# A decode kernel whose MLP and attention results are summed in one PSUM: biases by small matmuls, gates folded into the operands, last V load in two halves, one output transfer

## The chip, the cores and the metric

The kernel runs on 1 core of one Trainium2 chip. The metric is device time in microseconds (us). All runs here are of state "fast", so they can be compared with each other.

## The reference

A gated mix of one decode step of attention and an MLP, for 8 sequences of one token each:

```python
# B=8, Sq=1, D=576, H=32, Sk=4096, Dh=128, F=4608, all inputs bf16
g = sigmoid((x * gate_w).sum(-1, keepdims=True))
q = (x @ wq) per head;  p = softmax(q . k_cache * Dh**-0.5);  a = (p . v_cache) @ wo
h = gelu(layernorm(x) @ w1 + b1);                             b = h @ w2 + b2
out = g * a + (1 - g) * b
```

The K and V caches are 268 MB each. Everything else is small: 4.7 MB each for wq and wo, 5.3 MB each for w1 and w2.

## The kernel before

SBUF has three large slots of 64 KB per partition. wq, w1 and w2 are loaded into them first. Then come K and V of 32 groups (8 heads of one sequence each) in rotation, and at the end wo. All large loads are issued on one queue, and each load waits until its slot is free:

```python
land[kind, g] = op("sync", lambda e: e.dma_start(slot[s][:, :, :], src), free[n - 3], dma=dma)
# free after: up-projection (slot 1), down-projection (slot 2), scores of a group (K), eviction of O (V)
```

The MLP runs once, ahead of the first group. Its biases are broadcast to 8 partitions in four column quarters by eight small transfers, and VectorE adds them:

```python
ld_b1 = [load("scalar", b1_4[32 * i:32 * i + B, :], bcast(B_b1, i * FC, FC), ...) for i in range(4)]
ld_b2 = [load("scalar", b2_4[32 * i:32 * i + B, :], bcast(B_b2, i * QN, QN), ...) for i in range(4)]
for k in range(3):
    for c in range(4):                      # column group c of TensorE: PSUM partitions 32c..32c+7
        for kt in range(NKT):               # 5 matmuls, 8 columns of weights, 384 of data
            matmul(up_ps[k][32 * c:32 * c + B, 0:FB], lhsT=yT_sb[:, yi, :], rhs=w1..., start=(kt == 0), stop=(kt == NKT - 1))
    hb = up_ps[k] + b1_4; ...               # GELU in three parts
...
bmg = (y_ps + b2_4) * (1 - g)               # MLP result, kept in SBUF
```

A group then goes through scores (VectorE multiplies, TensorE sums), softmax, exponentials, 64 PV matmuls, eviction, row sums and gather, normalisation, and a copy into OT. (PV is the product of the softmax weights P with V; eviction is the copy of its result O from PSUM to SBUF; OT holds O of all groups, transposed for the product with wo.) The end of the kernel is:

```python
pv(last); evict(last); gather(last)         # gather begins with the row sums
norm(last)                                  # sum, reciprocal, On, OTs
place_o("vector", last - 1, last + 1)       # OT
for j in range(NJO):                        # 32 x 4 matmuls with wo, which arrives in pieces of 24, 6 and 2 j
    p_a = quarters(OT[:, j, :], wo_sb[:, j, :], j == 0, j == NJO - 1, [ld_wo[j], ...])
out_sb = y_ps * g4[:, 0:1] + bmg_sb         # one VectorE instruction on 104 partitions
ld_out = [load(("sync", "scalar")[i % 2], out_flat[:, i * QN:(i + 1) * QN], out_sb[32 * i:32 * i + B, :], ...) for i in range(4)]
```

## Time and profile before

| | before |
|---|---|
| time, median of the first three runs | 1296.77 us (1296.72 to 1297.39) |
| span of the profiled run | 1295.0 us |
| bytes moved, mean rate | 557.22 MB, 430 GB/s |
| busy share: TensorE, VectorE, ScalarE | 56%, 63%, 12% |

These are the lines of part 2 of the page. Each line has 40 slices of the span, and a digit is the busy share in tenths:

```profile
PE   2366466455556555556555556555556555556645
DVE  3387667655667665567665567765567765567762
DMA  9999999999999999999999999999999999999998
```

No compute engine is near full, and the DMA is at 9 tenths in all slices but the last. The loop is set by bytes: a change can gain only where the DMA stream is held up, and after it has ended.

The next lines are the end of the timeline. The columns are start in us, duration, engine, line, operation, tiles, count, and in brackets the idle time before it and what ended it:

```profile
1280.36 6.01 PE L617 MATMUL PS<-SL,P 128*32 128x512 bf16 x64 [2.67 <-DMA SL<-in_A_v_cache_dram]
1286.43 0.60 ACT L623 ACTIVATE O_sb<-PS 128x512 f32<-128x512 f32 x1 [10.82 <-PE PS L617]
...
1287.16 1.04 PE L632 MATMUL PS<-O_sb,selq 128*32 128x128 f32 x8
...
1289.72 2.17 PE L525 MATMUL PS<-SL,OT 128*8 128x144 bf16 x128 [1.51 <-DVE OT L656]
1291.94 0.37 DVE L727 SCALAR_TENSOR_TENSOR out_sb<-PS,g,bmg_sb 104x144 bf16<-104x144 f32 x1 [2.37 <-PE PS L525]
1292.34 0.72 SPq L320 DMA_DIRECT2D out_dram<-out_sb  x2
1292.34 0.65 ACTq L320 DMA_DIRECT2D out_dram<-out_sb  x2
```

This is a chain from the landing of the last V (1280.3) to the output. The 128 matmuls with wo were released by OT, which is compute. The chain does not show how close the wo load was behind. In the trace's landing records (when a transfer's semaphore tells that its data are there), the last of wo's three pieces landed at 1291.33, only 0.58 us before those matmuls were done.

In the prologue, the up-projection of the kernel before:

```profile
27.91 5.25 PE L496 MATMUL PS<-SL 128*8 128x384 bf16 x60 [7.79 <-DMA SL<-in_B_w_dram]
```

### The profile page before, as it was taken

To read this page: it belongs to the slowest core of one execution; us is meant where nothing else is said; L and a number is where in the kernel's file an instruction comes from. 1 tells how busy PE (TensorE), PEld (TensorE's weight loads), DVE (VectorE), ACT (ScalarE), POOL (GpSimd) and SP (SyncE) were. 2 spreads that over 40 slices of the span, in tenths; PEclk is the share of its full clock that TensorE was granted. 3 is DMA by queue.
4 is the path that set the end of the run, shared out by engine and by line. 5 is a ranking of instruction groups with operands and counts; after the bars stand their busy time and mean duration, and the time that the engine had idled before them with its cause. 6 is when DMAs were issued, how large, how long until landed. Compare 5 with 4: busy or idle time off the path is not lost.

```text
span 1295.0 us, 11764 instructions
## 1 busy us (share of the span) xinstructions
PE 720.0 (56%) x4902; PEld 333.8 (26%) x4902; DVE 821.5 (63%) x884; ACT 160.9 (12%) x587; POOL 41.0 (3%) x60
## 2 busy tenths in 40 slices
PE   2366466455556555556555556555556555556645
PEld 1222223122223122223222223222223222223223
DVE  3387667655667665567665567765567765567762
ACT  1011110111110111110011110011111011111011
POOL 1001000000000000000000000000000000000000
PEclk8698888877898787899788899878888877888888
DMA  9999999999999999999999999999999999999998
GB/s 395 437 428 440 430 436 430 433 435 433 433 431 435 437 429 433 433 435 437 425 437 435 433 431 431 437 435 431 435 429 437 435 427 435 435 435 431 429 439 343
DMA packets 10605, 557.22 MB, mean 430 GB/s; under 512 B 1328, under 2 KB 1344, under 8 KB 1888
## 3 DMA queue, kind: packets, MB, share of 16 engines
q1 hardware_dynamic: 10400, 556.93, 99.5%
q8 instruction: 9, 0.15, 0.0%
q10 hardware_dynamic: 192, 0.11, 0.0%
q14 instruction: 4, 0.03, 0.0%
HBM read 557.03 MB, written 0.01 MB: 430 GB/s over the span
## 4 chain that ended last, share of the span: by engine, by line
DMA 57%; DVE 23%; PE 13%; ACT 5%; issue 1%; ACTq 0%; SPq 0%
DMA SL<-in_A_k_cache_dram 53%; DVE SL L561 19%; PE PS L566 7%; PE PS L617 5%; ACT P L606 4%; DVE s_sb L572 4%; DMA SL<-in_A_v_cache_dram 3%; DMA SL<-in_A_wq_dram 1%; PE PS L632 1%; ACT O_sb L623 1%; PE PS L478 0%; PE PS L628 0%; PE PS L525 0%; SPq L320 0%; DVE OTs L646 0%
## 5 line engine op out<-in xcount | busy, mean ns | idle before, releaser
L566 PE MATMUL PS<-SL,ident 128*128 128x512 bf16 x2048 | 546.9, 419 | 530.3 <-DVE SL L561 530.3
L561 DVE TENSOR_TENSOR SL<-SL,q_bc 128x4096 bf16<-128x4096 bf16 x256 | 581.5, 2282 | 320.6 <-DMA SL<-in_A_k_cache_dram 320.6
L566 PEld LDWEIGHTS PS<-SL,ident 128*128 128x128 bf16 x2048 | 198.9, 106 | 865.3 <-DVE SL L561 627.4
L572 DVE TENSOR_REDUCE s_sb<-PS 128x32 f32<-128x512 f32 x256 | 175.1, 684 | 89.9 <-PE PS L566 89.7
L606 ACT ACTIVATE P<-s_sb,hb 128x256 bf16<-128x256 f32 x256 | 126.2, 494 | 663.2 <-PE PS L617 645.6
L617 PE MATMUL PS<-SL,P 128*32 128x512 bf16 x2048 | 127.9, 387 | 2.7 <-DMA SL<-in_A_v_cache_dram 2.7
L617 PEld LDWEIGHTS PS<-SL,P 128*32 128x32 bf16 x2048 | 95.8, 152 | 21.1 <-DMA SL<-in_A_v_cache_dram 3.1
L545 POOL TENSOR_SCALAR Qm<-Q,sel 128x256 bf16<-128x256 bf16 x33 | 34.2, 1036 | 908.1 <-ACT O_sb L623 845.4
L553 ACT ACTIVATE q_bc<-PS 128x128 bf16<-128x128 f32 x33 | 9.2, 278 | 418.2 <-PE PS L550 418.2
L606 ACT ACTIVATION_READ_ACCUMULATOR P<-s_sb,hb 128x1 f32 x256 | 47.8, 187 | 0.0
L632 PE MATMUL PS<-O_sb,selq 128*32 128x128 f32 x256 | 34.1, 278 | 0.0
L632 PEld LDWEIGHTS PS<-O_sb,selq 128*32 128x32 f32 x256 | 26.1, 113 | 0.2
L623 ACT ACTIVATE O_sb<-PS 128x512 f32<-128x512 f32 x32 | 18.4, 575 | 10.8 <-PE PS L617 10.8
L639 DVE TENSOR_REDUCE zs<-PS 32x1 f32<-32x8 f32 x32 | 4.7, 147 | 17.3 <-PE PS L632 17.3
L591 DVE TENSOR_REDUCE mA<-s_sb 128x1 f32<-128x256 f32 x32 | 13.4, 420 | 1.1
L656 POOL CAST OT<-OTs 32x96 bf16<-32x96 f32 (+2 forms) x12 | 3.8, 319 | 320.2 <-DVE OTs L646 320.1
L646 DVE TENSOR_REDUCE OTs<-On 32x32 f32<-32x128 f32 x32 | 11.9, 371 | 1.1
L642 DVE SCALAR_TENSOR_TENSOR On<-PS,rz,dqm 32x128 f32<-32x128 f32 x32 | 10.8, 339 | 1.2
L500 DVE TENSOR_TENSOR SL<-PS,SL 104x384 f32<-104x384 f32 x3 | 1.7, 552 | 15.3 <-PE PS L496 15.3
L628 PE MATMUL PS<-acc,hsel 128*32 128x8 f32 x64 | 7.4, 187 | 5.4 <-ACT O_sb L623 5.4
L496 PE MATMUL PS<-SL 128*8 128x384 bf16 x60 | 5.2, 492 | 7.8 <-DMA SL<-in_B_w_dram 7.8
L628 PEld LDWEIGHTS PS<-acc,hsel 128*32 128x32 f32 x64 | 4.4, 109 | 19.0 <-issue 12.7
(72 smaller groups left out, 107.9 us busy)
## 6 DMA issues: line engine op xcount, KB each, us to landing
SL<-in_B_w_dram SPq DMA_DIRECT2D x1, 5184.0 KB, 38.2
SL<-in_B_w_dram SPq DMA_DIRECT2D x1, 4608.0 KB, 24.6
SL<-in_A_wq_dram SPq DMA_DIRECT2D x1, 4096.0 KB, 13.0
SL<-in_A_wo_dram SPq DMA_DIRECT2D x1, 3456.0 KB, 21.9
SL<-in_A_wo_dram SPq DMA_DIRECT2D x1, 864.0 KB, 23.6
SL<-in_B_w_dram SPq DMA_DIRECT2D x1, 576.0 KB, 25.6
SL<-in_A_wq_dram SPq DMA_DIRECT2D x1, 512.0 KB, 14.2
SL<-in_A_k_cache_dram SPq DMA_DIRECT2D x32, 43.4
```

What stands on the lines that cost most here:

```text
L545: g_qm[g] = op("gpsimd", lambda e: e.tensor_scalar(out=Qm[:, :, :].rearrange("p k d -> p (k d)"), in0=Q4[:, 2 * hg * DH:(2 * hg + 2) * DH] ...
L561: v_mult[g, c] = op("vector", lambda e: e.tensor_tensor(out=part, in0=part, in1=qb, op=ALU.mult), [land["k", g], a_qb[g]], token="tensor" ...
L566: p_sum[g, c] = op("tensor", lambda e, r=r, n=n: e.matmul(tr_ps[par][:, :], lhsT=ident[:, :], rhs=r, start=(n == 0), stop=(n == NCH - 1)), ...
L572: v_red[g, c] = op("vector", lambda e: e.tensor_reduce(out=s_sb[:, c * CT:(c + 1) * CT], in_=tr_ps[par][:, :].rearrange("p (t c) -> p t c" ...
L591: t = op("vector", lambda e: e.tensor_reduce(out=mA[:, 0:1], in_=s_sb[:, :], axis=AX.X, op=ALU.max), [v_red[g, NCK - 1], c_mA], token=own)
L606: a_exp[g] = op("scalar", lambda e, h=h: e.activation(out=P[:, h, :], in_=s_sb[:, :], func=ACT.Exp, bias=hb8[:, h:h + 1], scale=1.0, accum ...
L617: p_pv[g] = op("tensor", lambda e, o=o, tq=tq: e.matmul(o, lhsT=P[:, :, :].rearrange("p h t -> p (h t)")[:, tq::NTQ], rhs=vb[:, tq::NTQ, : ...
L623: a_ev[g] = op("scalar", lambda e: e.activation(out=O_sb[:].rearrange("p t d -> p (t d)"), in_=o_ps[:, :], func=ACT.Copy), [p_pv[g], p_z.g ...
L628: p_z[g] = op("tensor", lambda e: e.matmul(oz_ps[0:32, DH:DH + HB], lhsT=hsel[:, :], rhs=acc[:, place(g), :], start=True, stop=True), [a_e ...
L632: p_oz[g] = op("tensor", lambda e, tt=tt: e.matmul(oz_ps[0:32, 0:DH], lhsT=selq[:, tt, :], rhs=O_sb[:, tt, :], start=(tt == 0), stop=(tt = ...
L642: t = op("vector", lambda e: e.scalar_tensor_tensor(out=On[:, :].rearrange("p (q j) -> p q j", q=NDQ), in0=oz_ps[0:32, 0:DH].rearrange("p ...
L646: v_norm[g] = op("vector", lambda e: e.tensor_reduce(out=OTs[:, :, place(g + 2)], in_=On[:, :].rearrange("p (q j) -> p j q", q=NDQ), axis= ...
```

## The change

Intent: take work off the end. The MLP stays in PSUM, and attention is added to it there. To allow that, (1-g) is folded into h, and g into O when OT is made. One evicted tile then goes out in one transfer. b1 enters as matmuls with a single row; b2, still broadcast to 8 partitions but in one transfer, enters as four fp32 matmuls that apply (1-g). So two small transfers take the place of the eight. The last V comes in two halves, so that its PV can begin early, and the row sums of the last group are made before its PV.

```diff
-    ld_b1 = [load("scalar", b1_4[32 * i:32 * i + B, :], bcast(B_b1, i * FC, FC), f"ld_b1{i}", [c_b1]) for i in range(4)]
-    ld_b2 = [load("scalar", b2_4[32 * i:32 * i + B, :], bcast(B_b2, i * QN, QN), f"ld_b2{i}", [c_b2]) for i in range(4)]
+    ld_b1 = load("scalar", b1_row, <one row of F>, "ld_b1")
+    ld_b2 = load("scalar", b2_8, bcast(B_b2, 0, D), "ld_b2")
...
+        if (kind, g) == ("v", NG - 1):
+            land[kind, g] = [<two loads, one per half>]
...
     for k in range(3):
         for c in range(4):
             for kt in range(NKT):
-                ... start=(kt == 0), stop=(kt == NKT - 1))
+                ... start=(kt == 0), stop=False)
-        <bias add and GELU of this third on VectorE>
+            p_up = op("tensor", lambda e, o=o, col=col: e.matmul(
+                o, lhsT=one1[:, :], rhs=b1_row[:, col:col + FB], start=False, stop=True), [ld_b1, c_one1])
+    <GELU of all 1152 columns at once, last factor times g4[0:QP, 1:2]>
...
+    for i in range(4):      # b2 times (1-g), fp32, into the same PSUM
+        p_b2 = matmul(y_ps[32 * i:32 * i + B, 0:QN], lhsT=diag2[:, 1, :], rhs=b2_f[:, i * QN:(i + 1) * QN], start=False, stop=False)
-    v_bx = ...; v_bmg = ...
...
+    row_sums(last); inverse(last)
     pv(last); evict(last); gather(last); norm(last); place_o("vector", last - 1, last + 1)    # place_o multiplies by g32
-        p_a = quarters(OT[:, j, :], wo_sb[:, j, :], j == 0, j == NJO - 1, ...)
+        p_a = quarters(OT[:, j, :], wo_sb[:, j, :], False, j == NJO - 1, ...)
+    parts = <four copies PSUM to out_sb [8, 576], two on VectorE, two on ScalarE>
+    ld_out = [load("sync", out_flat, out_sb[:, :], "ld_out", parts)]
```

(Cut. The exponentials also write P in two halves of the keys, so that the first 32 PV matmuls need only the first half of V.)

More of the change, by code (lines that the diff above doesn't have):

```diff
@@ L264, in bass_gated_mix__mha_block_cached__mixer_channel_mlp__decode_kernel @@
     late = Tail(2, NJ * D)
-    b1_4 = late.take([128, FC])
+    b1_row = late.take([1, F])
     hrow = late.take([128, FC])
     hT_sb = late.take([128, NJ, B])
-    hb = late.take32([128, FC])
+    b2_8 = late.take([B, D])
+    b2_f = late.take32([B, D])
     t2 = late.take32([128, FC])
-    b2_4 = sb("b2_4", [128, QN], BF16)
     Q4 = sb("Q4", [128, (H // 4) * DH], BF16)
@@ L284, in bass_gated_mix__mha_block_cached__mixer_channel_mlp__decode_kernel @@
     OT = sb("OT", [128, NJO, B], BF16)
-    bmg_sb = sb("bmg_sb", [128, QN], F32)
-    out_sb = sb("out_sb", [128, QN], BF16)
+    out_sb = sb("out_sb", [B, D], BF16)
+    spread8 = sb("spread8", [B, 128], F32)
+    ones8 = sb("ones8", [B, 32], F32)
+    one1 = sb("one1", [1, B], BF16)
+    diag2 = sb("diag2", [B, 2, B], F32)
     g4 = sb("g4", [128, 2], F32)
+    g32 = sb("g32", [32, 2, B], F32)
     ident = sb("ident", [128, 128], BF16)
@@ L298, in bass_gated_mix__mha_block_cached__mixer_channel_mlp__decode_kernel @@
     hb8 = sb("hb8", [128, HB], F32)
-    P = sb("P", [128, HB, NTT], BF16)
+    P = sb("P", [128, 2, HB, NTT // 2], BF16)
     O_sb = sb("O_sb", [128, TQ, DH], F32)
@@ L310, in bass_gated_mix__mha_block_cached__mixer_channel_mlp__decode_kernel @@
     y_ps = bank[7]
-    up_ps = [bank[4], bank[5], bank[6]]
+    up_ps = PS[:, 4 * 512:7 * 512].rearrange("p (k n) -> p k n", k=3)
+    g4_ps = bank[3][:, 0:2]
+    g32_ps = bank[3][0:32, 64:64 + 2 * B]
     ht_ps = PS[:, 0:NJ * 32].rearrange("p (j c b) -> p j c b", j=NJ, c=4)
@@ L339, in bass_gated_mix__mha_block_cached__mixer_channel_mlp__decode_kernel @@
     ld_w2 = load("sync", w2_sb, B_w2.rearrange("(p j) n -> p j n", j=NJ), "ld_w2")
-    c_b2 = op("gpsimd", lambda e: e.memset(b2_4[:], 0.0))
-    c_g4 = op("gpsimd", lambda e: e.memset(g4[:], 0.0))
-    c_b1 = op("gpsimd", lambda e: e.memset(b1_4, 0.0))
     ld_x = load("scalar", x_sb, x_flat, "ld_x")
     ld_gw = load("scalar", gw8, bcast(gate_w, 0, D), "ld_gw")
-    ld_b1 = [load("scalar", b1_4[32 * i:32 * i + B, :], bcast(B_b1, i * FC, FC), f"ld_b1{i}", [c_b1]) for i in range(4)]
-    ld_b2 = [load("scalar", b2_4[32 * i:32 * i + B, :], bcast(B_b2, i * QN, QN), f"ld_b2{i}", [c_b2]) for i in range(4)]
+    ld_b1 = load("scalar", b1_row, bass.AP(tensor=B_b1.tensor, offset=B_b1.offset, ap=[[F, 1], [1, F]]), "ld_b1")
+    ld_b2 = load("scalar", b2_8, bcast(B_b2, 0, D), "ld_b2")
     def kv_src(cache, g):
@@ L370, in load_kv @@
         used_in = g if kind == "k" else g + 1
+        if (kind, g) == ("v", NG - 1):
+            land[kind, g] = [load("sync", slot[s][:, i * NTT // 2:(i + 1) * NTT // 2, :],
+                                  src[:, i * NTT // 2:(i + 1) * NTT // 2, :], f"ld_v{g}_{i}", free[n - 3]) for i in range(2)]
+            return n
         if in_loop(used_in):
@@ L377, in load_kv @@
         land[kind, g] = op("sync", lambda e: e.dma_start(slot[s][:, :, :], src), free[n - 3], dma=dma)
+        if kind == "v":
+            land[kind, g] = [land[kind, g]] * 2
         return n
@@ L410, in bass_gated_mix__mha_block_cached__mixer_channel_mlp__decode_kernel @@
         in_=bass.AP(tensor=sel32, offset=0, ap=[[pstride(sel32), 128], [1, TQ], [TQ, HB], [0, NDQ]])), [c_sel32])
+    c_one8 = memset("gpsimd", ones8[:], 1.0)
+    c_one1 = memset("gpsimd", one1[:], 1.0)
+    c_b2 = op("gpsimd", lambda e: e.tensor_copy(out=b2_f, in_=b2_8), [ld_b2])
+    c_sp8 = op("vector", lambda e: e.tensor_copy(
+        out=spread8[:].rearrange("b (c r) -> b c r", c=4),
+        in_=bass.AP(tensor=ident, offset=0, ap=[[pstride(ident), B], [0, 4], [1, 32]])), [c_id])
     c_Rows = op("vector", lambda e: e.tensor_reduce(
@@ L461, in bass_gated_mix__mha_block_cached__mixer_channel_mlp__decode_kernel @@
                                                    scalar1=-1.0, scalar2=1.0, op0=ALU.mult, op1=ALU.add), [a_g])
-    for i in range(4):
-        v_g4 = op("vector", lambda e, i=i: e.tensor_copy(out=g4[32 * i:32 * i + B, :], in_=stat[:, G_COL:G_COL + 2]),
-                  [v_omg, c_g4])
+    v_dg = op("vector", lambda e: e.tensor_tensor(
+        out=diag2[:], in0=bass.AP(tensor=ident, offset=0, ap=[[pstride(ident), B], [0, 2], [1, B]]),
+        in1=bass.AP(tensor=stat, offset=G_COL, ap=[[pstride(stat), B], [1, 2], [0, B]]), op=ALU.mult), [v_omg, c_id])
     v_yz = spread(yz, y_sb, [v_y])
@@ L467, in bass_gated_mix__mha_block_cached__mixer_channel_mlp__decode_kernel @@
     v_yT = untransposed(yT_sb, YT_COL, [p_yT])
+    t = op("tensor", lambda e: e.matmul(g4_ps, lhsT=spread8[:, :], rhs=stat[:, G_COL:G_COL + 2], start=True, stop=True),
+           [v_dg, c_sp8])
+    t = op("tensor", lambda e: e.matmul(g32_ps, lhsT=ones8[:, :], rhs=diag2[:].rearrange("k s b -> k (s b)"),
+                                        start=True, stop=True), [c_one8])
+    v_g4 = op("vector", lambda e: e.tensor_copy(out=g4[:, :], in_=g4_ps), [t])
+    v_g32 = op("vector", lambda e: e.tensor_copy(out=g32[:].rearrange("p s b -> p (s b)"), in_=g32_ps), [t])
     a_Q = []
@@ L484, in bass_gated_mix__mha_block_cached__mixer_channel_mlp__decode_kernel @@
     load_kv("k", 0)
-    v_hb, v_hrow = [], []
     for k in range(3):
-        p_up = None
         for c in range(4):
+            col = c * FC + k * FB
+            o = up_ps[32 * c:32 * c + B, k, 0:FB]
             for kt in range(NKT):
-                o = up_ps[k][32 * c:32 * c + B, 0:FB]
-                col = c * FC + k * FB
                 r = w1_sb[:, kt, col:col + FB] if kt < NKF else w1_t[:, col - (c // 2) * (F // 2):][:, 0:FB]
@@ L496, in bass_gated_mix__mha_block_cached__mixer_channel_mlp__decode_kernel @@
                 p_up = op("tensor", lambda e, o=o, r=r, kt=kt, yi=yi: e.matmul(
-                    o, lhsT=yT_sb[:, yi, :], rhs=r, start=(kt == 0), stop=(kt == NKT - 1)),
+                    o, lhsT=yT_sb[:, yi, :], rhs=r, start=(kt == 0), stop=False),
                     [v_yT, *ld_w1, *c_ps] if c == kt == k == 0 else ())
-        cs = slice(k * FB, (k + 1) * FB)
-        v_hb.append(op("vector", lambda e, k=k, cs=cs: e.tensor_tensor(
-            out=hb[0:QP, cs], in0=up_ps[k][0:QP, 0:FB], in1=b1_4[0:QP, cs], op=ALU.add), [p_up, *ld_b1]))
@@ L502, in bass_gated_mix__mha_block_cached__mixer_channel_mlp__decode_kernel @@
-        t = op("vector", lambda e, cs=cs: e.tensor_tensor(out=t2[0:QP, cs], in0=hb[0:QP, cs], in1=hb[0:QP, cs],
-                                                          op=ALU.mult), [v_hb[k]])
-        t = op("vector", lambda e, cs=cs: e.tensor_scalar(out=t2[0:QP, cs], in0=t2[0:QP, cs], scalar1=0.044715,
-                                                          scalar2=1.0, op0=ALU.mult, op1=ALU.add), [t])
-        t = op("vector", lambda e, cs=cs: e.tensor_tensor(out=t2[0:QP, cs], in0=t2[0:QP, cs], in1=hb[0:QP, cs],
-                                                          op=ALU.mult), [t])
@@ L508, in bass_gated_mix__mha_block_cached__mixer_channel_mlp__decode_kernel @@
-        t = op("scalar", lambda e, cs=cs: e.activation(out=t2[0:QP, cs], in_=t2[0:QP, cs], func=ACT.Sigmoid,
-                                                       scale=gelu_c), [t])
-        v_hrow.append(op("vector", lambda e, cs=cs: e.tensor_tensor(
-            out=hrow[0:QP, cs], in0=hb[0:QP, cs], in1=t2[0:QP, cs], op=ALU.mult), [t]))
-    free[1] = [p_up]
+            p_up = op("tensor", lambda e, o=o, col=col: e.matmul(
+                o, lhsT=one1[:, :], rhs=b1_row[:, col:col + FB], start=False, stop=True), [ld_b1, c_one1])
@@ new lines, in bass_gated_mix__mha_block_cached__mixer_channel_mlp__decode_kernel @@
+    free[1] = [p_up]
+    h = up_ps[0:QP, :, 0:FB]
+    t3 = t2[0:QP, :].rearrange("p (k n) -> p k n", k=3)
+    t = op("vector", lambda e: e.tensor_copy(out=t3, in_=h), [p_up])
+    t = op("vector", lambda e: e.tensor_tensor(out=t3, in0=t3, in1=h, op=ALU.mult), [t])
+    t = op("vector", lambda e: e.tensor_scalar(out=t3, in0=t3, scalar1=0.044715, scalar2=1.0, op0=ALU.mult, op1=ALU.add), [t])
+    t = op("vector", lambda e: e.tensor_tensor(out=t3, in0=t3, in1=h, op=ALU.mult), [t])
+    t = op("scalar", lambda e: e.activation(out=t3, in_=t3, func=ACT.Sigmoid, scale=gelu_c), [t])
@@ L514, in bass_gated_mix__mha_block_cached__mixer_channel_mlp__decode_kernel @@
+    v_h = op("vector", lambda e: e.scalar_tensor_tensor(
+        out=hrow[0:QP, :].rearrange("p (k n) -> p k n", k=3), in0=h, scalar=g4[0:QP, 1:2], in1=t3,
+        op0=ALU.mult, op1=ALU.mult), [t, v_g4])
+    v_hb, v_hrow = [v_h], [v_h]
     per_quarter = bass.AP(tensor=ident, offset=0, ap=[[pstride(ident), QP], [32, 4], [1, B]])
@@ L530, in bass_gated_mix__mha_block_cached__mixer_channel_mlp__decode_kernel @@
     for jt in range(NJ):
-        p_down = quarters(hT_sb[:, jt, :], w2_sb[:, jt, :], jt == 0, jt == NJ - 1,
+        p_down = quarters(hT_sb[:, jt, :], w2_sb[:, jt, :], jt == 0, False,
                           [ld_w2, *v_hT, v_yT] if jt == 0 else ())
-    v_bx = op("vector", lambda e: e.tensor_tensor(
-        out=bmg_sb[0:QP, :], in0=y_ps[0:QP, 0:QN], in1=b2_4[0:QP, :], op=ALU.add), [p_down, *ld_b2])
-    v_bmg = op("vector", lambda e: e.tensor_scalar(
-        out=bmg_sb[0:QP, :], in0=bmg_sb[0:QP, :], scalar1=g4[0:QP, 1:2], scalar2=None, op0=ALU.mult), [v_bx, v_g4])
-    free[2] = [p_down]
-    a_qb, v_mult, v_red, p_sum, v_nm, a_exp, p_pv, a_ev, p_z, p_oz, v_norm, g_ot, g_qm, p_q = ({} for _ in range(14))
+    for i in range(4):
+        p_b2 = op("tensor", lambda e, i=i: e.matmul(
+            y_ps[32 * i:32 * i + B, 0:QN], lhsT=diag2[:, 1, :], rhs=b2_f[:, i * QN:(i + 1) * QN], start=False, stop=False),
+            [c_b2, v_dg])
+    free[2] = [p_b2]
+    a_qb, v_mult, v_red, p_sum, v_nm, a_exp, p_pv, a_ev, p_z, p_oz, v_norm, g_ot, g_qm, p_q, v_rz = ({} for _ in range(15))
     def q_of(g):
@@ L606, in exps @@
             a_exp[g] = op("scalar", lambda e, h=h: e.activation(
-                out=P[:, h, :], in_=s_sb[:, :], func=ACT.Exp, bias=hb8[:, h:h + 1], scale=1.0,
+                out=P[:, :, h, :], in_=s_sb[:, :].rearrange("p (s t) -> p s t", s=2), func=ACT.Exp, bias=hb8[:, h:h + 1], scale=1.0,
                 accum_out=acc[:, place(g), h:h + 1]),
@@ L613, in pv @@
         vb = slot[at_slot["v", g]]
+        flat = P[:, :, :, :].rearrange("p s h t -> p (s h t)")
         for tq in range(NTQ):
+            s, i = divmod(tq, NTQ // 2)
             o = o_ps[32 * (tq % 4):32 * (tq % 4) + TQ * HB, :]
-            w = [land["v", g], a_exp[g] if g < G0 - 1 else a_ev[g - 1], a_ev.get(g - 1), *v_hT] if tq == 0 else ()
-            p_pv[g] = op("tensor", lambda e, o=o, tq=tq: e.matmul(
-                o, lhsT=P[:, :, :].rearrange("p h t -> p (h t)")[:, tq::NTQ], rhs=vb[:, tq::NTQ, :],
-                start=(tq < 4), stop=(tq >= NTQ - 4)), w,
+            lhsT = flat[:, s * HB * NTT // 2 + i:(s + 1) * HB * NTT // 2:NTQ // 2]
+            rhs = vb[:, s * NTT // 2 + i:(s + 1) * NTT // 2:NTQ // 2, :]
+            w = [land["v", g][s], a_exp[g] if g < G0 - 1 else a_ev[g - 1], a_ev.get(g - 1), *v_hT] if i == 0 else ()
+            p_pv[g] = op("tensor", lambda e, o=o, lhsT=lhsT, rhs=rhs, tq=tq: e.matmul(
+                o, lhsT=lhsT, rhs=rhs, start=(tq < 4), stop=(tq >= NTQ - 4)), w,
                 token="scalar" if in_loop(g + 1) and tq == NTQ - 1 else None)
@@ L624, in evict, with row_sums @@
                                                       func=ACT.Copy), [p_pv[g], p_z.get(g - 1)])
+    def row_sums(g):
+        p_z[g] = op("tensor", lambda e: e.matmul(
+            oz_ps[0:32, DH:DH + HB], lhsT=hsel[:, :], rhs=acc[:, place(g), :], start=True, stop=True),
+            [a_ev[g] if g < NG - 1 else a_ev[g - 1], v_norm.get(g - 1), c_hsel, *v_hb])
     def gather(g):
         looped = in_loop(g + 2)
-        p_z[g] = op("tensor", lambda e: e.matmul(
-            oz_ps[0:32, DH:DH + HB], lhsT=hsel[:, :], rhs=acc[:, place(g), :], start=True, stop=True),
-            [a_ev[g], v_norm.get(g - 1), c_hsel, *v_hb])
         for tt in range(TQ):
@@ L633, in gather, with inverse @@
                 oz_ps[0:32, 0:DH], lhsT=selq[:, tt, :], rhs=O_sb[:, tt, :], start=(tt == 0),
-                stop=(tt == TQ - 1)), [c_selq] if tt == 0 else (),
+                stop=(tt == TQ - 1)), [a_ev[g], c_selq, v_rz.get(g)] if tt == 0 else (),
                 token="vector" if looped and tt == TQ - 1 else None)
+    def inverse(g):
+        own = "vector" if in_loop(g + 2) else None
+        t = op("vector", lambda e: e.tensor_reduce(out=zs[:, :], in_=oz_ps[0:32, DH:DH + HB], axis=AX.X, op=ALU.add),
+               [p_oz.get(g, p_z[g])], token=own)
+        v_rz[g] = op("vector", lambda e: e.reciprocal(out=rz[0:32, :], in_=zs[:, :]), [t], token=own)
     def norm(g):
         own = "vector" if in_loop(g + 2) else None
-        t = op("vector", lambda e: e.tensor_reduce(out=zs[:, :], in_=oz_ps[0:32, DH:DH + HB], axis=AX.X, op=ALU.add),
-               [p_oz[g]], token=own)
-        t = op("vector", lambda e: e.reciprocal(out=rz[0:32, :], in_=zs[:, :]), [t], token=own)
         t = op("vector", lambda e: e.scalar_tensor_tensor(
@@ L644, in norm @@
             scalar=rz[0:32, 0:1], in1=bass.AP(tensor=dqm, offset=0, ap=[[pstride(dqm), 32], [1, NDQ], [0, NJO]]),
-            op0=ALU.mult, op1=ALU.mult), [t, c_dqm], token=own)
+            op0=ALU.mult, op1=ALU.mult), [v_rz[g], p_oz[g], c_dqm], token=own)
         v_norm[g] = op("vector", lambda e: e.tensor_reduce(
@@ L655, in place_o @@
             n = min(g1 - g, B - b)
-            t = g_ot[g0] = op(engine, lambda e, hg=hg, b=b, n=n, at=g - g0: e.tensor_copy(
-                out=OT[32 * hg:32 * hg + 32, :, b:b + n], in_=OTs[:, :, at:at + n]), [v_norm[g1 - 1], t])
+            t = g_ot[g0] = op(engine, lambda e, hg=hg, b=b, n=n, at=g - g0: e.tensor_tensor(
+                out=OT[32 * hg:32 * hg + 32, :, b:b + n], in0=OTs[:, :, at:at + n],
+                in1=bass.AP(tensor=g32, offset=b, ap=[[pstride(g32), 32], [0, NJO], [1, n]]), op=ALU.mult),
+                [v_norm[g1 - 1], v_g32, t])
             g += n
@@ L696, in bass_gated_mix__mha_block_cached__mixer_channel_mlp__decode_kernel @@
         if in_loop(g):
+            row_sums(g - 2)
             gather(g - 2)
@@ L706, in bass_gated_mix__mha_block_cached__mixer_channel_mlp__decode_kernel @@
         if in_loop(g):
+            inverse(g - 2)
             norm(g - 2)
@@ L716, in bass_gated_mix__mha_block_cached__mixer_channel_mlp__decode_kernel @@
     last = NG - 1
+    row_sums(last - 1)
     gather(last - 1)
+    inverse(last - 1)
     norm(last - 1)
+    row_sums(last)
+    inverse(last)
     pv(last)
@@ L724, in bass_gated_mix__mha_block_cached__mixer_channel_mlp__decode_kernel @@
     for j in range(NJO):
-        p_a = quarters(OT[:, j, :], wo_sb[:, j, :], j == 0, j == NJO - 1,
-                       [ld_wo[j], v_bx, *g_ot.values()])
-    t = op("vector", lambda e: e.scalar_tensor_tensor(
-        out=out_sb[0:QP, :], in0=y_ps[0:QP, 0:QN], scalar=g4[0:QP, 0:1], in1=bmg_sb[0:QP, :],
-        op0=ALU.mult, op1=ALU.add), [p_a, v_bmg])
-    ld_out = [load(("sync", "scalar")[i % 2], out_flat[:, i * QN:(i + 1) * QN], out_sb[32 * i:32 * i + B, :],
-                   f"ld_out{i}", [t]) for i in range(4)]
+        p_a = quarters(OT[:, j, :], wo_sb[:, j, :], False, j == NJO - 1, [ld_wo[j], *g_ot.values()])
+    parts = [op("vector" if i < 2 else "scalar", lambda e, i=i: (e.tensor_copy if i < 2 else e.copy)(
+        out_sb[:, i * QN:(i + 1) * QN], y_ps[32 * i:32 * i + B, 0:QN]), [p_a]) for i in range(4)]
+    ld_out = [load("sync", out_flat, out_sb[:, :], "ld_out", parts)]
     op("sync", lambda e: None, ld_out)
```

## The prediction

> What bounds the kernel: the DMA. In the page's 40 slices its share is 9 tenths nearly throughout, 430 GB/s over a span of 1295.0 us; TensorE is 56% busy, VectorE 63%. The DMA queue's waits show the next K or V load always issued while an earlier one is still moving (last K: issued at 1198.4, landed at 1241.6). So the 32 loop passes are set by bytes, and the change leaves those bytes alone. Only the start and the end can move the time.
>
> Start. Up-projection, GELU and down-projection run from 27.9 to 49.2 us in the timeline, but the first K lands only at 60.45, so some 10 us are slack. The 12 bias matmuls, the joined 1152-column VectorE chain and 4 fp32 matmuls for b2 may add about 4 us: hidden. The V load that waits for the down-projection has 30 us of slack. The broadcast bias rows go from 64 packets to a few: at most 0.4 us of some engines' time (2304-byte packets took about 0.095 us each, 32 of them on a part of the engines), so 0 to 0.4 us of the stream's end.
>
> End, from the timeline and the chain of waits: last V landed 1280.32; 64 PV matmuls to 1286.4, mostly at half clock; eviction 0.61; row sums 0.23; gather 0.91; sum and reciprocal 0.37; On, OTs, OT 0.95; Wo matmuls 1289.72 to 1291.91; output 0.37; four output transfers; end 1295.0. The chain names these steps, so on paper V in halves and early row sums take off 1.5 to 3 us (the first half should land about 9.7 us earlier, so TensorE can start once the head before has been gathered and normalised, about 1279). But Wo's three pieces land at 1288.57, 1290.64 and 1291.33 (DMA landings in the trace), just behind the chain. They queue behind V and do not come earlier. So Wo's matmuls can't finish before about 1291.5, and the new chain turns into a wait for Wo: nearly all the gain of the halves is lost, 0.4 us at most remain.
>
> Worse, TensorE will now idle 1.5 to 3 us before Wo's first piece. The Trainium skill, TensorE: Matmul & The Clock Gate, Part 1, says the clock is judged over free-running windows of about 3.4 us and halves after an idle one; here the granted clock was 0.50 from 1274.9 to 1285.1 (three such windows) and 1.0 after. If it falls again, Wo's 128 matmuls cost 31 ns each (as the down-projection's 144 did, 4.49 us) instead of 17, and end near 1292.5: 0.6 us later than now.
>
> Output: two VectorE copies in parallel with two ScalarE copies of 8x144, estimated at 0.5 us against 0.37 now; one transfer saves the second issue on each queue, 0.35 to 0.4 us (first transfers landed 1293.55 and 1293.76, second ones 1293.96 and 1294.16). Net about -0.25 us.
>
> Sum: -0.25 (output), 0 to -0.4 (start), -0.4 to +0.6 (Wo at full or half clock): about -0.6 us of 1296.77. Predicted 1296.2 us, range 1295.2 to 1297.2; faster by over 2% 0.005, within 2% 0.99, slower 0.005.
>
> What would show it: DMA slices unchanged; the chain's end names the Wo load ahead of the last matmuls; PV ends 1 to 2.5 us earlier while Wo's matmuls start at the landing of Wo's first piece (about 1288.6); one output transfer. Wrong if Wo lands earlier or later with V in halves, if the second half of V waits for something new, if the strided P slows PV inside the loop (slack about 13 us per V load), or if the HBM rate differs between runs by more than 0.1%.

## The result, and the profile after

The median was 1295.3 us (six runs, 1294.77 to 1296.44), against 1297.1 us for the kernel before in the same rounds (1296.72 to 1297.62). The ratio is 0.9987, 95% interval 0.9974 to 1.0: by the 2% verdict the same, by the sign about 1.7 us faster; all six runs lie below the fastest of the kernel before. A ratio is the mean time of one kernel's fast runs over that of the other's fast runs of the same rounds, so it is not quite the ratio of the medians quoted. The six runs fall in two sets: 1294.77, 1294.80, 1294.81 and 1295.80, 1295.95, 1296.44. The profiled run is one of the fast set, with a span of 1293.2 us.

The end of the timeline after:

```profile
1277.68 6.53 PE L640 MATMUL PS<-SL,P 128*32 128x512 bf16 x61
...
1284.92 1.06 PE L656 MATMUL PS<-O_sb,selq 128*32 128x128 f32 x8 [0.71 <-ACT O_sb L645]
...
1287.36 1.68 PE L544 MATMUL PS<-SL,OT 128*8 128x144 bf16 x96 [1.38 <-DMA SL<-in_A_wo_dram]
1289.46 0.55 PE L544 MATMUL PS<-SL,OT 128*8 128x144 bf16 x24 [0.43 <-DMA SL<-in_A_wo_dram]
1290.22 0.30 PE L544 MATMUL PS<-SL,OT 128*8 128x144 bf16 x8 [0.21 <-DMA SL<-in_A_wo_dram]
1290.57 0.57 ACT L761 CAST out_sb<-PS 8x144 bf16<-8x144 f32 x2 [5.70 <-PE PS L544]
1290.57 0.63 DVE L761 CAST out_sb<-PS 8x144 bf16<-8x144 f32 x2 [3.50 <-PE PS L544]
1291.23 0.37 SPq L326 DMA_DIRECT2D out_dram<-out_sb  x1
```

The bracket of the wo matmuls is the reading to take. Before, "OT" ended their wait; now the wo load does, three times, once per piece. The chain of waits says the same. Its last pieces (start, duration, what):

```profile
1266.17 24.00 DMA SL<-in_A_wo_dram
...
1290.22 0.33 PE PS L544 x8
```

The table below splits the 1.88 us between the two profiled spans (1295.05 and 1293.17) at points of the timeline and the landing records:

| | before | after | difference |
|---|---|---|---|
| last landing of wo | 1291.33 | 1290.18 | -1.15 |
| from there to the end of the last wo matmul | 0.58 | 0.37 | -0.21 |
| from there to the first output issue | 0.43 | 0.68 | +0.25 |
| from there to the end of the span | 2.71 | 1.94 | -0.77 |

More than half is the first line: the load stream itself ended earlier, though hardly any bytes were taken from it. To find where, I summed the bytes that all packets had moved up to a given time (each packet's bytes spread evenly over its own time), divided by 430 GB/s, and compared the traces. The reference is the kernel `e2_best` of the second call below, a run without a disturbance of the stream. A negative number means that the trace is behind it by so many us:

```
time (us)   before   after
   10        0.03    -0.04
   15       -0.67    -0.04
   20       -0.73    -0.04
  110       -0.74    -0.05
 1250       -0.77    -0.04
```

The kernel before lost 0.7 us of its stream between 10 and 15 us from the start and never again. The rest of the 1.15 us is the spread among the DMA engines. The 16 increments of the last piece's semaphore came between 1288.89 and 1291.33 before, and between 1288.33 and 1290.18 after. The Trainium skill (DMA: Bandwidth & Descriptors, "Why a DMA increments its semaphore by 16 and not by 1") says that a transfer runs on up to 16 engines "that finish independently", and these records agree. A landing is that of the slowest engine.

The up-projection after, where the five matmuls of a column group alternate with one bias matmul (the first two and the last two of twelve rounds):

```profile
27.34 1.76 PE L515 MATMUL PS<-SL 128*8 128x384 bf16 x5 [6.75 <-DMA SL<-in_B_w_dram]
29.02 0.48 PE L518 MATMUL PS<-SL,one 1*8 1x384 bf16 x1
29.43 1.69 PE L515 MATMUL PS<-SL 128*8 128x384 bf16 x5
31.05 0.32 PE L518 MATMUL PS<-SL,one 1*8 1x384 bf16 x1
...
41.71 0.98 PE L515 MATMUL PS<-SL 128*8 128x384 bf16 x5
42.61 0.32 PE L518 MATMUL PS<-SL,one 1*8 1x384 bf16 x1
```

It took 15.6 us (27.34 to 42.93) instead of 5.25. The first two rounds ran at half clock (until 30.91 us), the last ten at full clock. There the starts within a group of five lie 163 ns apart, one after the other, and the starts before and after each bias matmul 0.25 us. And VectorE's first multiplication, in the kernel before and in the changed one:

```profile
60.47 4.49 DVE L561 TENSOR_TENSOR SL<-SL,q_bc 128x4096 bf16<-128x4096 bf16 x2 [10.43 <-DMA SL<-in_A_k_cache_dram]
...
59.89 4.49 DVE L580 TENSOR_TENSOR SL<-SL,q_bc 128x4096 bf16<-128x4096 bf16 x2 [5.06 <-DMA SL<-in_A_k_cache_dram]
```

After the change the first q was there at 59.78 (its copy started at 59.50 and took 0.28), and the first K at 59.82; before, q was there at 49.70. The slack of the prologue is used up to the last 0.04 us in this run.

### The profile page after: what moved, and what is told of

Its sections match the earlier page's. It is cut to its first block, busy times and chain, and to the rows that moved or that the text cites. A ratio compares the mean times of both kernels' runs of the same rounds, so it can differ in the third digit from the quotient of the medians.

```text
span 1293.2 us, 11790 instructions
## 1 busy us (share of the span) xinstructions
PE 733.4 (57%) x4926; PEld 337.1 (26%) x4926; DVE 819.7 (63%) x873; ACT 161.0 (12%) x587; POOL 40.4 (3%) x60
## 4 chain that ended last, share of the span: by engine, by line
DMA 54%; DVE 26%; PE 14%; ACT 5%; issue 1%; SPq 0%; ACTq 0%; DVEq 0%
DMA SL<-in_A_k_cache_dram 50%; DVE SL L580 20%; PE PS L585 7%; DVE s_sb L591 5%; ACT P L625 4%; PE PS L640 4%; DMA SL<-in_B_w_dram 2%; DMA SL<-in_A_wo_dram 2%; PE PS L515 1%; PE PS L656 1%; ACT O_sb L645 1%; PE PS L544 0%; PE PS L518 0%; PE PS L649 0%; PE PS L535 0%
## 5 line engine op out<-in xcount | busy, mean ns | idle before, releaser
L515 PE MATMUL PS<-SL 128*8 128x384 bf16 x60 | 13.2, 356 | 6.8 <-DMA SL<-in_B_w_dram 6.8
L683 POOL TENSOR_TENSOR OT<-OTs,g 32x96 bf16<-32x96 f32 (+2 forms) x12 | 4.2, 347 | 320.3 <-DVE OTs L673 320.2
```

The lines of the kernel that those rows point to most:

```text
L515: p_up = op("tensor", lambda e, o=o, r=r, kt=kt, yi=yi: e.matmul(o, lhsT=yT_sb[:, yi, :], rhs=r, start=(kt == 0), stop=False), [v_yT, *ld_ ...
```

## The experiments

Theories about the gain (B, H against W, O) and about the scatter (C, T/S) were to be told apart.

- **B**: the eight small broadcast transfers held up the stream at the start.
- **H**: the halves of V carry the gain.
- **W**, against H: wo's landing sets the end, so the halves bring nothing.
- **O**: one transfer instead of four saves time at the end.
- **C**: the scatter is TensorE's clock at the wo matmuls.
- **T/S**, formed after the first call: the slowed up-projection delays the first pass, and the DMA queue runs dry later.

### First call: parts of the change undone

The changed kernel unaltered, as the measure:

> The changed kernel once more, unaltered, as the measure for the others of this call. All theories: about 1.8 us under the kernel before (as on record: 1295.3 against 1297.1), single runs scattered between 1294.8 and 1296.4. Theory C (the scatter is the TensorE clock at the Wo matmuls): if the granted clock is 0.5 when Wo's first piece lands, Wo's matmuls take about 31 ns each instead of 17 and the run belongs to the slow end.

The last V in one load:

```diff
-        if (kind, g) == ("v", NG - 1):
+        if False:
```

> The changed kernel with the last V loaded whole again; early row sums, one output transfer and the rest stay. Theory W (the end is set by the landing of Wo's last piece, the halves bring nothing by themselves): the PV matmuls end about 1 us later, at some 5 us after V's landing, Wo's matmuls start at most 1 us later, but the last one ends within 0.2 us of the same distance from Wo's last landing; time within 0.2 us of the unaltered changed kernel, or even a little faster if the shorter wait keeps the clock up. Rival H (the halves carry the gain, as the chain of waits of the kernel before suggests): 1 to 2 us slower than the unaltered changed kernel.

Four output transfers:

```diff
-    ld_out = [load("sync", out_flat, out_sb[:, :], "ld_out", parts)]
+    ld_out = [load(("sync", "scalar")[i % 2], out_flat[:, i * QN:(i + 1) * QN], out_sb[:, i * QN:(i + 1) * QN],
+                   f"ld_out{i}", parts) for i in range(4)]
```

> The changed kernel with four output transfers on two queues again, from the same result tile. Theory O (one transfer saves the second issue on each queue): 0.3 to 0.5 us slower than the unaltered changed kernel; in the profile, the span from the last Wo matmul to the end grows from 2.6 to about 3.0 us. Rival: no difference, the second issue is hidden, and the gain is all in the load stream.

The broadcast transfers added back, into memory that nothing reads:

```diff
+    ld_spare = [load("scalar", spare1[32 * i:32 * i + B, :], bcast(B_b1, i * FC, FC), ...) for i in range(4)]
+    ld_spare += [load("scalar", spare2[32 * i:32 * i + B, :], bcast(B_b2, i * QN, QN), ...) for i in range(4)]
-    free[2] = [p_b2]
+    free[2] = [p_b2, *ld_spare]
```

> The changed kernel with the eight broadcast transfers of the biases (64 small rows) added back, into spare memory that nothing reads. Theory B (those small transfers held up the load stream at the start): first K lands about 0.6 us later (60.4 instead of 59.8), Wo's last piece lands later by as much, time 0.4 to 0.8 us slower than the unaltered changed kernel. Rival N (the earlier landing is scatter of the stream from run to run): no difference beyond 0.2 us.

Measured, sorted, five runs each (the nine runs of before in these rounds: mean 1297.10):

| kernel | runs (us) | mean |
|---|---|---|
| e1_control | 1295.14 1295.18 1295.22 1295.51 1296.87 | 1295.58 |
| e1_one_v | 1294.61 1294.73 1295.88 1296.29 1296.87 | 1295.68 |
| e1_four_out | 1295.75 1296.16 1296.31 1297.33 1297.52 | 1296.61 |
| e1_bcast | 1295.75 1297.06 1297.60 1297.82 1298.72 | 1297.39 |

The scatter of one kernel is as large as most of the effects. The directions speak for W (whole V: no loss), O (four transfers: +1.0) and B (broadcasts: +1.8), but the last two are larger than expected and the table alone does not settle the sizes. The scatter had to be understood first.

The profiles did that. They happened to be of fast and slow runs, and VectorE's first multiplication differs in what it waited for. First the unaltered kernel's slow run (1296.87), then the slow run with the broadcasts (1297.82):

```profile
61.28 4.49 DVE L580 TENSOR_TENSOR SL<-SL,q_bc 128x4096 bf16<-128x4096 bf16 x2 [5.51 <-ACT q_bc L572]
```

```profile
65.64 4.49 DVE L584 TENSOR_TENSOR SL<-SL,q_bc 128x4096 bf16<-128x4096 bf16 x2 [5.60 <-ACT q_bc L576]
```

They waited for q, not for K: the MLP's delay had reached the critical path. In the slow run with the broadcasts, the up-projection ran its first five rounds at half clock. Two of its rounds:

```profile
28.77 1.76 PE L519 MATMUL PS<-SL 128*8 128x384 bf16 x5 [7.56 <-DMA SL<-in_B_w_dram]
30.46 0.48 PE L522 MATMUL PS<-SL,one 1*8 1x384 bf16 x1
```

A round takes 2.1 us so (28.77 to 30.86), against 1.16 us at full clock. The phase of the clock thus decides how late q is: without broadcasts, the whole stretch took 15.5 us in the profiled run of e2_warm (second call) and 19.3 us in that of e1_one_v, where the half clock lasted until 38.9 us and not 30.5. The delay is passed on (in the run with the broadcasts, q came 5.75 us later than in the run after, and the second V load 5.86 us), because VectorE works through the first two groups almost without a pause: the second V load, which waits for the scores of the second group, is issued later by as much. The DMA queue's timeline shows it for the run after, then for the slow run with the broadcasts:

```profile
84.42 0.33 SPq L384 DMA_DIRECT2D SL<-in_A_k_cache_dram  x1
111.47 0.33 SPq L384 DMA_DIRECT2D SL<-in_A_v_cache_dram  x1
```

```profile
90.47 0.33 SPq L388 DMA_DIRECT2D SL<-in_A_k_cache_dram  x1
117.33 0.33 SPq L388 DMA_DIRECT2D SL<-in_A_v_cache_dram  x1
```

The next lines give what the DMA did meanwhile, from the view of windows (the last two columns are DMA share and GB/s), for the same two kernels. The view books each packet wholly in the window in which it starts, so its figures are rough: a share over 1 comes from that.

```profile
115.00:120.00 5.00, 0.05 (x4) 0.00 (x0) 2.06 (x1) 4.52 (x17) 0.23 (x1) 0.97 1.08 462
```

```profile
115.00:120.00 5.00, 4.60 (x60) 2.67 (x64) 3.40 (x10) 0.00 (x0) 0.00 (x0) 1.00 0.79 279
```

So the queue ran dry, some 70 to 90 us after the cause (the up-projection, 28.8 to 48.1 us). With each packet spread over its own time, the engines were 28% busy between 117 and 118 us in the run with the broadcasts, and 100% in the run after. All traces with the alternation, and e3_delay, by the cumulative bytes (loss between 110 and 125 us):

```
                 second V load issued   stream lost, 110 to 125 us
e2_warm (below)       111.06                 0.00 us
after                 111.47                 0.00
e1_four_out           112.90                 0.06
e1_control            113.04                 0.19
e3_delay (below)      113.93                 0.66
e1_one_v              115.65                 1.34
e1_bcast              117.33                 2.09
```

(e1_one_v lost another 0.8 us between 150 and 200 us, which was not followed up.) The bytes are a mean over the engines. In e1_control and e3_delay some engines ran dry and others did not: the last V's (or its second half's) 16 increments spread over 3.4 us there, over 1.8 us in the run after. The last landing therefore suffers more than the mean.

Theory C has its place too. In e1_control's slow run the clock was at half when wo's first piece landed, and the wo matmuls, all 128 in one stretch, took 3.77 us:

```profile
1288.94 3.77 PE L544 MATMUL PS<-SL,OT 128*8 128x144 bf16 x128 [2.91 <-DMA SL<-in_A_wo_dram]
```

They ended 1.1 us after wo's last landing (1291.65), against 0.37 us in the run after.

### Second call: the remedies

Before, without its broadcast transfers (the biases stay zero, so the result is wrong):

```diff
-    ld_b1 = [load(...) for i in range(4)];  ld_b2 = [load(...) for i in range(4)]
+    ld_b1, ld_b2 = [c_b1], [c_b2]      # the memsets to zero
```

> The kernel before without its eight broadcast transfers of the biases; the bias tiles stay zero, so the result is wrong on purpose. Theory B: the load stream ends 0.4 to 0.8 us earlier (first K at about 59.8 instead of 60.45), and since Wo's last piece lands only 0.6 us ahead of the end of its matmuls and these wait for the PV chain, the whole chain moves with V: 0.4 to 0.8 us faster than the kernel before. Rival N: no difference beyond 0.2 us.

The bias matmuls after all the others:

```diff
-            p_up = <bias matmul of group (k, c)>          # inside the loops over k and c
+    for k in range(3):
+        for c in range(4):
+            p_up = <bias matmul of group (k, c)>          # after those loops
```

> The changed kernel with the twelve one-row bias matmuls after all sixty up-projection matmuls, not after each group of five. Theory T (a matmul with one row makes TensorE change its tiling, so the four column groups no longer run side by side): the up-projection falls from 15.6 us to about 6.5 us, the chain to the first q is ready near 50 instead of 59.5, and the time is unchanged within 0.2 us, because the first K lands at 59.8 anyway. Rival: the twelve extra matmuls are slow by themselves (some 0.8 us each), and the stretch stays near 15 us.

Filling matmuls while TensorE waits for wo:

```diff
     gather(last)
+    for i in range(5):
+        op("tensor", lambda e: e.matmul(bank[3][:, :], lhsT=ident[:, :], rhs=<512 columns of P>, start=True, stop=True))
     norm(last)
```

> The changed kernel with five 512-column matmuls on a free bank after the last gather, to keep TensorE busy until Wo lands. Theory C (the scatter of the changed kernel is the clock at Wo's matmuls): all runs at the fast end, scatter under 0.6 us, mean 0.3 to 0.6 us faster than the changed kernel in its own rounds. Rival (the scatter is that of the load stream): same mean and the same scatter as the changed kernel.

Both edits together:

> The changed kernel with both: bias matmuls last and the five filling matmuls. Theories T and C: time as the kernel with the filling matmuls alone, 2 us or more under the kernel before; up-projection near 6.5 us. Rival: as the changed kernel.

Measured (the nine runs of before in these rounds: mean 1297.25):

| kernel | runs (us) | mean |
|---|---|---|
| e2_before_nobias | 1295.30 1295.38 1295.62 1295.66 1295.87 | 1295.57 |
| e2_bias_last | 1294.73 1295.05 1295.06 1295.39 1295.46 | 1295.14 |
| e2_warm | 1294.48 1294.55 1294.68 1295.53 1295.73 | 1294.99 |
| e2_best | 1294.65 1294.74 1294.79 1294.86 1294.91 | 1294.79 |

*Theory B.* The kernel before without its broadcasts gains 1.7 us, about as much as the whole change and twice the upper end of what was expected. The bytes account for 0.9 us of it (0.12 us ahead of the reference at 125 us, where before is 0.74 us behind). In the two profiles the last wo landing moved by 1.23 us (1291.33 to 1290.10).

*Theory T.* The up-projection with the bias matmuls last, from the timeline:

```profile
27.23 5.16 PE L515 MATMUL PS<-SL 128*8 128x384 bf16 x60 [7.92 <-DMA SL<-in_B_w_dram]
32.31 0.66 PE L521 MATMUL PS<-SL,one 1*8 1x384 bf16 x12
```

The same 72 matmuls take 5.7 us instead of 15.6. The bias matmuls cost 0.7 us; it was the alternation that cost 10. A page of the Trainium skill names a possible reason (TensorEngine Tiling (Array Packing), section "Tiling Modes", Key Properties): "Changing tiling mode (not just tile) drains the TensorE". If a matmul of 1 row is in another mode than one of 128 rows, then between two drains only the five matmuls of one column group are left, and they go one after the other. That fits the starts: 163 ns apart within the five, 0.25 us before and after each bias matmul. That the mode is what differs is an inference from the page and was not tested; what the run shows is that the order alone costs 10 us and ends the overlap of the column groups. The expectation that the time would not change, "because the first K lands at 59.8 anyway", was met only in part. The mean is 0.4 us below e1_control's (another call), and no run reaches 1296; but only 2 of the 11 runs of the changed kernel did, so these five runs alone do not show that the long ones are gone.

*Theory C.* e2_warm alone did not meet its expectation of a scatter under 0.6 us: two of five runs are 1 us longer. The up-projection still alternates there, which may be why; the profile is of a fast run and does not show it. Together with the bias order (e2_best) the scatter falls to 0.26 us, and the mean lies 0.35 us under e2_bias_last of the same rounds. The profiled run of e2_bias_last had the half clock at wo and that of e2_best did not. The windows (the third number from the end is the granted clock), for e2_bias_last, and the timeline line of e2_best (96 matmuls in 1.67 us):

```profile
1288.50:1292.00 3.50, 2.69 (x88) 2.04 (x76) 0.59 (x2) 0.55 (x2) 0.00 (x0) 0.63 0.18 62
```

```profile
1287.29 1.67 PE L547 MATMUL PS<-SL,OT 128*8 128x144 bf16 x96 [1.87 <-DMA SL<-in_A_wo_dram]
```

### Third call: the parts again, on the quiet base

The same edits as in the first call, now on e2_best.

> The kernel with bias matmuls last and filling matmuls (the quiet base, 1294.65 to 1294.91), with the last V loaded whole. Theory W (Wo's landing sets the end, the halves bring next to nothing): 0 to 0.3 us slower than the base. Rival H: 1 to 2 us slower.

> The quiet base with four output transfers on two queues. Theory O: 0.3 to 0.6 us slower than the base, from the last transfer being issued 0.35 us later. Rival: within 0.1 us.

> The quiet base with the eight small broadcast transfers added back into unread memory. Theory B (they cost the load stream 0.7 us at 10 to 15 us from the start, as the bytes moved by then show for the kernel before): 0.5 to 0.8 us slower than the base, and no loss of bytes near 118 us, unlike the same edit without the bias matmuls last. Rival N: within 0.1 us.

And a delay on purpose, on e2_best:

```diff
+    for i in range(60):
+        op("tensor", lambda e: e.matmul(bank[3][:, :], lhsT=ident[:, :], rhs=w2_sb[:, 0, 0:512], start=True, stop=True), ...)
     for jt in range(NJ):
         p_down = quarters(...)
```

> The quiet base with sixty useless 512-column matmuls ahead of the down-projection, some 14 us, so that the first q is ready near 64.5 us instead of 50. Theory S (the late first pass delays the second V load past the point where the queue runs dry, at about 113 us): the second V load is issued at 115.5 to 117, the DMA moves fewer bytes between 115 and 120 us, the load stream is 1 to 3 us behind from then on, and the run is 1 to 3 us slower than the base. Rival (the prologue's slack hides it, and the scatter of the changed kernel comes from the memory): unchanged within 0.3 us.

Measured (the nine runs of before in these rounds: mean 1297.08; e2_best was run in the call before, on another chip, where before had 1297.25):

| kernel | runs (us) | mean | ratio to before |
|---|---|---|---|
| e2_best | 1294.65 1294.74 1294.79 1294.86 1294.91 | 1294.79 | 0.9981 |
| e3_one_v | 1294.47 1294.57 1294.58 1294.63 1294.63 | 1294.58 | 0.9981 |
| e3_four_out | 1295.72 1295.84 1295.88 1295.90 1295.93 | 1295.85 | 0.9990 |
| e3_bcast | 1295.66 1295.71 1295.97 1296.19 1296.29 | 1295.96 | 0.9992 |
| e3_delay | 1295.40 1295.73 1296.30 1296.74 1296.77 | 1296.19 | 0.9992 |

All five runs of e3_four_out, e3_bcast and e3_delay lie above all ten of e2_best and e3_one_v.

*W holds and H falls.* With the last V whole, the kernel is no slower; both have the ratio 0.9981. The evictions of e2_best and of e3_one_v, and the end of the latter's timeline:

```profile
1282.53 0.60 ACT L648 ACTIVATE O_sb<-PS 128x512 f32<-128x512 f32 x1 [8.30 <-PE PS L643]
1284.05 0.60 ACT L648 ACTIVATE O_sb<-PS 128x512 f32<-128x512 f32 x1 [9.81 <-PE PS L643]
...
1287.20 1.67 PE L547 MATMUL PS<-SL,OT 128*8 128x144 bf16 x96 [0.26 <-DMA SL<-in_A_wo_dram]
1289.30 0.99 PE L547 MATMUL PS<-SL,OT 128*8 128x144 bf16 x32 [0.42 <-DMA SL<-in_A_wo_dram]
```

Here too the wo matmuls wait for wo; the eviction comes later than in e2_best (1284.05 against 1282.53) and only the wait gets shorter (0.26 us against 1.87). The early row sums stayed in all these runs, so what they bring was not tested alone.

*O holds, and is larger than thought:* 1.1 to 1.3 us (against e2_best and e3_one_v) for 0.3 to 0.6 expected. The issues of the output, for e2_best and then for e3_four_out:

```profile
1291.41 0.37 SPq L326 DMA_DIRECT2D out_dram<-out_sb  x1
1291.36 0.65 ACTq L326 DMA_DIRECT2D out_dram<-out_sb  x2
1291.36 0.72 SPq L326 DMA_DIRECT2D out_dram<-out_sb  x2
```

In the profiles, from the first output issue to the last landing it is 1.82 us with four transfers and 1.35 us with one, and from there to the end of the span 0.91 and 0.59 us. Only the first part was reckoned with, and not even all of it. That accounts for 0.8 us; the rest of the difference in time lies outside what the spans show.

*B holds:* 1.2 to 1.4 us (0.5 to 0.8 expected). By the bytes, the stream is 0.88 us behind at 110 us, 0.65 us of which were lost between 10 and 15 us, and loses nothing near 118 us. What the broadcasts do to the stream stands in the packet records. The middle column spreads each packet over its own time:

```
                    GB/s, 12.5 to       mean time of the 128 packets of
                    14.5 us             4096 bytes (second load of wq)
before              309                 217 ns
after               424                 159
e3_bcast            322                 210
e2_before_nobias    426                 159
```

The engines were not idle meanwhile: in all four traces they were busy throughout these 2 us. The packets of the large loads took longer while the broadcast rows passed. Summed over all packets of the large loads that started between 11 and 18 us, the excess over the undisturbed times is 0.69 us before and 0.67 us in e3_bcast, shared by 16 engines. That is the size of the loss. The packets of all small transfers at the start, end markers included, took 6.2 us of engine time before and 2.3 after, a difference of 0.24 us when shared by 16 engines, so their own time does not explain 0.7 us. Why the large packets were slowed, by eight reads of the same row or by anything else, is not settled.

*S holds:* the useless matmuls delayed q to 62.06 us and the second V load to 113.93, less than planned since they ran mostly at full clock. The stream lost 0.66 us there, and the mean is 1.4 us up. The rival, that the memory scatters by itself, falls: with a quiet prologue the five runs of e2_best, of e3_one_v and of e3_four_out agree within 0.3 us each (those of e3_bcast, which disturb the start, within 0.63).

B and O together make 2.3 to 2.7 us, about the 2.5 us by which e2_best and e3_one_v lie under before. No large part of the gain is left without a cause.

Version to keep: e3_one_v (the bias matmuls last, five filling matmuls, the last V whole, the rest of the change as it is), 1294.58 us. All five of its runs lie below all eleven runs of the changed kernel (1294.77 to 1296.87) and 2.5 us below the mean of before in its rounds.

## Why the prediction was right or wrong

The measured 1295.3 us lies in the range 1295.2 to 1297.2, near its lower edge, and the class is the forecast one. The point, 1296.2, was 0.9 us too high. That the median fell into the range is in part luck, as two errors ran against each other. Point by point:

- *"The 32 loop passes are set by bytes."* Right. From 125 us on, the cumulative bytes of before and after stay apart by the same 0.7 us.
- *"The new chain turns into a wait for Wo: nearly all the gain of the halves is lost, 0.4 us at most remain."* Right. The chain of waits names the wo load, and loading V whole on the quiet base costs nothing. From wo's last landing to the last matmul, 0.21 us were gained. PV ended 2.2 us earlier and wo's matmuls started at the landing of its first piece, as said; but that landing came at 1287.3 and not "about 1288.6", since the stream ended earlier.
- *"So 0 to 0.4 us of the stream's end"* for the broadcast rows. The mechanism was right, the term was too small. It was sized by the small packets' own time; what it left out is that the large load's packets take longer beside them (217 ns against 159). The stream lost 0.7 us, and in time 1.2 to 1.4 us (e3_bcast) or 1.7 us (e2_before_nobias). By e2_before_nobias this is the largest part of the gain; by e3_bcast it is about as large as the output's.
- *"Net about -0.25 us"* for the output. Mis-sized: the profiles give -0.52 us (+0.25 for the four copies, -0.77 for the transfers and the end), and in time one transfer is worth 1.1 to 1.3 us against four. I counted only the later issue.
- *"May add about 4 us: hidden"* for the prologue. This step failed. The bias matmuls were reckoned as twelve more matmuls, but the alternation undoes the overlap of column groups and adds 10 us in the best trace. That used the whole slack, and at an unlucky clock phase the queue ran dry later, for up to 1.3 us (2.1 with the broadcasts added back). Of the traces with the alternation, those of e1_control, e1_one_v and e1_bcast show a loss of 0.19 us or more, and those of the changed kernel's first run, e1_four_out and e2_warm do not. The rest of the added work was hidden: in e2_best, with the bias matmuls in one block, q was there at 49.51, against 49.70 in the kernel before.
- *"If it falls again, Wo's 128 matmuls ... end near 1292.5: 0.6 us later."* It fell in some runs (e1_control, e2_bias_last) and not in others; in those two they ended 1.1 and 0.6 us after wo's last landing instead of 0.37 us.
- The two errors on the one side (start and output undersized) and the failed step on the other partly cancelled; this is the luck. A fast run of the changed kernel is at 1294.8, below the range.

## What to carry to other kernels

In a transfer-bound kernel like this one the gain lay at the ends: look for what holds up the stream in its first microseconds (small broadcast transfers did), for the last landing, and for what follows it (one output transfer instead of four), and not for compute that ends ahead of the last landing. Slack is a budget that several steps draw on, and overdrawing it may show only tens of microseconds later, as a queue that runs dry; scatter between runs of one kernel was such a sign here. Keep matmuls with few rows out of a stream that relies on column groups running side by side: do them in one block.

## What the Trainium skill lacked or had wrong

- TensorEngine Tiling (Array Packing): it says that a change of tiling mode drains TensorE, but gives no size. Here twelve one-row matmuls between groups of five cost 10 us (15.6 us against 5.7 us with the same matmuls in one block): the overlap of the column groups is gone, and the starts around each one-row matmul lie 0.25 us apart (163 ns within the five). That a drain is the reason is inferred.
- TensorE: Matmul & The Clock Gate, Part 1: its table has the clock halve "after ≥1 idle window". In these traces it halved after a window that was not idle: busy 1.32 us of 3.4 (before, 18.8 to 22.2 us) and 0.53 us of 3.4 (e1_control, 1285.5 to 1288.9 us). It stayed at full speed after 1.67 us of 3.4 (after, 1283.6 to 1287.0 us), but halved after 1.78 us (after, 41.15 to 44.56 us), so the busy time in the trace does not give a sharp limit. (Part 1 also tells of a clock that oscillates when TensorE idles briefly and often, without a figure for how much idling that takes.)
- DMA: Bandwidth & Descriptors: it explains why small descriptors are slow themselves, not that they slow others. Here eight small broadcast transfers beside a large load cost the stream 0.7 us, where the packets' own time explains 0.24 us; packets of 4096 bytes of the large load took 217 ns beside them instead of 159. No page has this.
- No page has the cost of splitting a last output transfer: four instead of one took 0.47 us more from issue to landing and 0.32 us more from there to the end of the span.
